# Two chained attentions and a gated MLP on one core: the first softmax's sums taken as a tiled product, its scale applied to the packed rows, and new instruction lists

## The chip, the cores and the metric

The kernel runs on one core of one Trainium2 chip. A core has five engines with a list of instructions each: TensorE (PE: matmuls, with its weight loads shown as PEld), VectorE (DVE), ScalarE (ACT), GpSimd (POOL) and SyncE (SP, which here issues nearly all DMAs). An engine works through its list strictly in order and waits at semaphores for what others produce. SBUF is the on-chip memory with 128 partitions; PSUM holds matmul results in banks of 512 float32 columns. The metric is the device time of one execution in microseconds (us), the median of several runs.

## The reference

Shapes: batch 8, heads 8, sequence 576, head size 64, 32 packed queries p per head; MLP 512 to 2048 to 512.

```python
def sm_attn(qq, kk, vv):
    s = scale * np.matmul(qq, kk.transpose(0, 1, 3, 2))
    s = s - np.max(s, axis=-1, keepdims=True)
    a = np.exp(s)
    a = a / (np.sum(a, axis=-1, keepdims=True) + 1e-09)
    return np.matmul(a, vv)
p_packed = sm_attn(p, k, v)
out = sm_attn(q, p_packed, p_packed)

h = x @ w_in
g = h * (1.0 / (1.0 + np.exp(-beta * h)))
return (g @ w_out).astype(np.float32)
```

Here x is the attention's output with the heads of one token laid side by side. In the first attention 32 packed queries look at 576 keys; in the second, 576 queries look at the 32 packed rows, which serve as keys and as values.

## The kernel before

The work goes batch by batch, b from 0 to 7. In the lists below, each entry is a step: a name, the batch, and an index.

For each batch: `cast` turns k, v and q into bfloat16; `tr` and `trr` transpose k and q, on TensorE for batches 0 and 1 and by a DMA for the later ones; `s1` and `s1r` are the first scores, with the keys on the partitions; `e1` and `e1r` are their exponentials, kept in `E1T`. A tile of `E1T` has 256 columns: the 8 heads by 32 packed queries, in the order (r, c, j), where head = 2c + r and j is the query. `z1` adds the exponentials over the keys and `i1` inverts the sums. `pun` multiplies v by the exponentials (its result is `pp_ps`); `pp` brings that to SBUF as bfloat16, still without the division by the sums. `s2` (and `s2r` for the 64 remaining tokens) are the second scores from `pp` and q; `e2`, `e2r` their exponentials; `z2`, `l2`, `n2` and `A2` divide by the second sums, by a logarithm and an exponential on ScalarE and a product on VectorE.

The product of `pp` with w_in is taken before the second attention is applied: `w` (b, n), n from 0 to 3, multiplies a quarter of w_in by `pp`, and `W` (b, m) scales the result with beta into `W_bf`. Then `h` is one 128-row block of the hidden layer (two matmuls of 512 columns), `g` its SiLU, `hr` and `gr` the same for the remaining 64 tokens. `o` is the last product for batches 0 and 1 and for the remaining rows; for batches 2 to 7 the last product is done by seven block products instead of eight (`p` and `P` on TensorE, the sums `S` on VectorE, the reads `R..` on VectorE and ScalarE). `take` and `add` bring results to SBUF; `store` writes them out.

`z1` before takes the exponentials as the stationary operand, 128 of the 256 columns at a time, and one column of ones as the moving operand. Its result is a column for r = 0 and one for r = 1, with a sum on each partition (c, j). In that form the inverse of a sum is a value per partition for everything that has (c, j) on its partitions: the second scores and the product `w`. So `e2` and `e2r` take it (times 1/8) as ScalarE's scale operand, L695 and L700, and `W` takes it as the scalar of a three-operand instruction, L795.

The `s2`, `s2r` and `w` matmuls use the array as eight tiles of 64 rows by 32 columns (`pos=` gives the tile); everything else uses it whole. A run of neighbouring steps of the tiled kind is called a burst here.

What order the work has is written out by hand in `SEQUENCE`, one list of steps for each of the five engines. The `Planner` doesn't choose the order; it runs through the lists with assumed durations, and uses them for one thing alone: in the first 60 us, where it reckons that TensorE would stand still, it puts in "fill" matmuls, which multiply an identity by itself and whose result nobody reads (`keep_warm`, shown as o_ps<-identr). `TILED` names the steps that the planner takes for tiled.

PSUM banks are shared: `h` and `o` have two each, and all attention steps (s1, z1, pun, s2, z2, w) take turns in four. Weights w_in and w_out arrive in blocks of 1 MB through three staging slots: a block's load is issued when the casts of the third block before it are done. SP's list holds the loads, the DMA transposes and the stores in one order.

All matmuls are recorded at one line, that of the helper `mm` (L382), and PE transposes at L387, so the profile tells them apart by tile names: z_ps<-ones,E1T is z1, z_ps<-E2T,bones is z2, s_ps<-qT,pp is s2, s_ps<-pT,kT is s1, pp_ps is pun.

Of the kernel before, what the change touches and what calls it, by code (L numbers as in the profile page):

```python
# [21 lines left out]
NC = 4  # L22
# [22 lines left out]
TILED = {"w": 1, "s2": 1}  # L45
# [22 lines left out]
        ("o", 0, 3, 9), ("o", 0, 3, 11), ("s2", 1, 1), ("w", 1, 1), ("o", 0, 2, 9), ("o", 0, 3, 13), ("z2", 1, 2),
        ("o", 0, 2, 11), ("w", 1, 2), ("o", 0, 2, 13), ("h", 1, 2), ("o", 0, 2, 15), ("h", 1, 1), ("o", 0, 3, 15),
        ("h", 1, 0), ("w", 1, 3), ("h", 1, 5), ("h", 1, 3), ("p_tr", 1), ("h", 1, 4), ("o", 1, 0, 1), ("h", 1, 11),  # L70
        ("p_tr", 0), ("h", 1, 6), ("o", 1, 0, 3), ("h", 1, 8), ("o", 1, 1, 1), ("h", 1, 9), ("h", 1, 10),
        ("o", 1, 1, 3), ("hr", 0, 0), ("h", 1, 7), ("o", 1, 0, 5), ("o", 1, 1, 5), ("s1r", 2), ("hr", 0, 1),
        ("s1", 2, 1), ("o", 1, 0, 7), ("s1", 2, 0), ("h", 1, 15), ("o", 1, 0, 9), ("o", 1, 0, 11), ("o", 1, 1, 7),
        ("z1", 2), ("pun", 2, 0), ("o", 1, 1, 9), ("pun", 2), ("o", 1, 1, 11), ("h", 1, 13), ("h", 1, 12),
        ("w", 2, 0), ("w", 2, 1), ("h", 1, 14), ("o", 1, 1, 13), ("hr", 1, 0), ("o", 1, 0, 13), ("o", 1, 0, 15),
        ("hr", 1, 1), ("o", 1, 1, 15), ("s2", 2, 0), ("w", 2, 2), ("o", 1, 2, 1), ("o", 1, 2, 3), ("z2", 2, 0),
        ("o", 1, 2, 5), ("z2", 2, 1), ("o", 1, 3, 1), ("s2", 2, 1), ("o", 1, 2, 7), ("o", 1, 2, 9), ("o", 1, 3, 3),
        ("o", 1, 2, 11), ("o", 1, 2, 13), ("o", 1, 2, 15), ("o", 1, 3, 5), ("o", 1, 3, 7), ("z2", 2, 2), ("h", 2, 0),
        ("h", 2, 6), ("o", 1, 3, 9), ("s1r", 3), ("o", 1, 3, 11), ("h", 2, 1), ("s1", 3, 1), ("o", 1, 4, 1),
        ("o", 1, 3, 13), ("s1", 3, 0), ("o", 1, 4, 3), ("w", 2, 3), ("o", 1, 4, 5), ("o", 1, 4, 7), ("h", 2, 2),  # L80
        ("o", 1, 4, 9), ("o", 1, 3, 15), ("z1", 3), ("pun", 3, 0), ("h", 2, 7), ("h", 2, 3), ("pun", 3),
        ("o", 1, 4, 11), ("h", 2, 8), ("h", 2, 11), ("w", 3, 0), ("w", 3, 1), ("h", 2, 9), ("h", 2, 10),
        ("o", 1, 4, 13), ("o", 1, 4, 15), ("h", 2, 5), ("h", 2, 13), ("w", 3, 2), ("w", 3, 3), ("h", 2, 4),
        ("h", 2, 12), ("p", 2, 1, 0), ("p", 2, 1, 1), ("h", 2, 15), ("h", 2, 14), ("p", 2, 1, 2), ("P", 2, 1),
        ("hr", 2, 0), ("p", 2, 2, 0), ("hr", 2, 1), ("p", 2, 2, 1), ("p", 2, 2, 2), ("s2", 3, 0), ("s2", 3, 1),
        ("P", 2, 2), ("p", 2, 6, 0), ("p", 2, 6, 1), ("z2", 3, 0), ("p", 2, 6, 2), ("P", 2, 6), ("z2", 3, 1),
        ("z2", 3, 2), ("p", 2, 5, 0), ("p", 2, 5, 1), ("s1r", 4), ("s1", 4, 1), ("p", 2, 5, 2), ("s1", 4, 0),
        ("P", 2, 5), ("p", 2, 7, 0), ("p", 2, 7, 1), ("p", 2, 7, 2), ("P", 2, 7), ("p", 2, 3, 0), ("h", 3, 15),
        ("p", 2, 3, 1), ("z1", 4), ("h", 3, 14), ("p", 2, 3, 2), ("h", 3, 1), ("pun", 4, 0), ("h", 3, 0),
        ("p", 2, 4, 0), ("h", 3, 9), ("P", 2, 3), ("h", 3, 8), ("pun", 4), ("p", 2, 4, 1), ("h", 3, 5), ("h", 3, 2),  # L90
        ("w", 4, 0), ("w", 4, 1), ("h", 3, 3), ("h", 3, 7), ("p", 2, 4, 2), ("P", 2, 4), ("h", 3, 11), ("h", 3, 10),
        ("w", 4, 2), ("w", 4, 3), ("h", 3, 4), ("h", 3, 6), ("p", 3, 1, 0), ("p", 3, 1, 1), ("h", 3, 13),
        ("h", 3, 12), ("p", 3, 1, 2), ("P", 3, 1), ("p", 3, 2, 0), ("p", 3, 2, 1), ("hr", 3, 0), ("p", 3, 2, 2),
        ("hr", 3, 1), ("P", 3, 2), ("s2", 4, 0), ("s2", 4, 1), ("p", 3, 6, 0), ("p", 3, 6, 1), ("p", 3, 6, 2),
        ("z2", 4, 0), ("p", 3, 5, 0), ("P", 3, 6), ("z2", 4, 1), ("p", 3, 5, 1), ("p", 3, 5, 2), ("z2", 4, 2),
        ("P", 3, 5), ("s1r", 5), ("s1", 5, 0), ("s1", 5, 1), ("p", 3, 7, 0), ("p", 3, 7, 1), ("h", 4, 10),
        ("p", 3, 7, 2), ("P", 3, 7), ("z1", 5), ("pun", 5, 0), ("p", 3, 3, 0), ("p", 3, 4, 0), ("p", 3, 4, 1),
        ("h", 4, 7), ("h", 4, 2), ("p", 3, 3, 1), ("pun", 5), ("p", 3, 3, 2), ("h", 4, 14), ("h", 4, 15),
        ("p", 3, 4, 2), ("P", 3, 3), ("h", 4, 0), ("h", 4, 1), ("P", 3, 4), ("w", 5, 0), ("w", 5, 1), ("h", 4, 11),
        ("h", 4, 12), ("o", 3, 4, 1), ("o", 3, 4, 3), ("h", 4, 13), ("h", 4, 8), ("o", 3, 4, 5), ("o", 3, 4, 7),  # L100
        ("h", 4, 3), ("h", 4, 6), ("w", 5, 2), ("w", 5, 3), ("hr", 4, 0), ("h", 4, 4), ("o", 3, 4, 9),
        ("o", 3, 4, 11), ("h", 4, 9), ("h", 4, 5), ("o", 3, 4, 13), ("o", 3, 4, 15), ("s2", 5, 0), ("s2", 5, 1),
        ("p", 4, 1, 0), ("p", 4, 1, 1), ("p", 4, 1, 2), ("hr", 4, 1), ("z2", 5, 0), ("P", 4, 1), ("p", 4, 2, 0),
        ("z2", 5, 1), ("p", 4, 2, 1), ("p", 4, 2, 2), ("P", 4, 2), ("p", 4, 6, 0), ("p", 4, 6, 1), ("p", 4, 6, 2),
        ("P", 4, 6), ("p", 4, 5, 0), ("h", 5, 10), ("h", 5, 11), ("p", 4, 5, 1), ("p", 4, 5, 2), ("h", 5, 7),
        ("h", 5, 3), ("P", 4, 5), ("p", 4, 7, 0), ("p", 4, 7, 1), ("z2", 5, 2), ("s1r", 6), ("p", 4, 7, 2),
        ("s1", 6, 0), ("p", 4, 3, 0), ("s1", 6, 1), ("p", 4, 3, 1), ("P", 4, 7), ("p", 4, 3, 2), ("h", 5, 15),
        ("h", 5, 13), ("P", 4, 3), ("p", 4, 4, 0), ("p", 4, 4, 1), ("h", 5, 9), ("h", 5, 1), ("p", 4, 4, 2),
        ("z1", 6), ("h", 5, 8), ("h", 5, 0), ("pun", 6, 0), ("pun", 6), ("h", 5, 2), ("h", 5, 14), ("w", 6, 0),
        ("w", 6, 1), ("h", 5, 4), ("h", 5, 5), ("P", 4, 4), ("w", 6, 2), ("h", 5, 6), ("h", 5, 12), ("p", 5, 1, 0),  # L110
        ("p", 5, 1, 1), ("hr", 5, 0), ("hr", 5, 1), ("w", 6, 3), ("s2", 6, 0), ("p", 5, 1, 2), ("P", 5, 1),
        ("p", 5, 2, 0), ("p", 5, 2, 1), ("p", 5, 2, 2), ("P", 5, 2), ("z2", 6, 0), ("s2", 6, 1), ("p", 5, 6, 0),
        ("p", 5, 6, 1), ("p", 5, 6, 2), ("z2", 6, 1), ("P", 5, 6), ("z2", 6, 2), ("s1r", 7), ("s1", 7, 0),
        ("p", 5, 5, 0), ("p", 5, 5, 1), ("s1", 7, 1), ("p", 5, 5, 2), ("p", 5, 7, 0), ("p", 5, 7, 1), ("p", 5, 7, 2),
        ("P", 5, 5), ("h", 6, 2), ("h", 6, 12), ("P", 5, 7), ("p", 5, 3, 0), ("p", 5, 3, 1), ("h", 6, 4),
# [235 lines left out]
class Kernel:  # L351
# [153 lines left out]
    def plan_attention(self, b):  # L505
# [838 lines left out]
```

## Time and profile before

| what | value |
|---|---|
| median of 3 runs (lowest, highest) | 246.91 us (246.82, 247.11) |
| the profiled execution's time | 246.91 us |
| its span, first to last instruction | 245.1 us |
| granted TensorE clock, mean | 1.000 |
| busy: PE, ACT, DVE, POOL | 231.1, 178.8, 148.7, 58.8 us |
| bytes moved by DMA | 54.13 MB, mean 221 GB/s |
| fill matmuls (o_ps<-identr) | 132, 11.7 us busy |

The profile's page has first the busy time of each engine, then the span in 40 slices of some 6.1 us with a digit for the busy tenths of each; then the DMA queues, the chain of waits that ended last, and the costliest groups of instructions (line, engine, operation, output<-inputs, shape, count; then busy us, mean ns of one, and the idle time before them with what ended it). The timeline lists instructions in order of time, equal neighbours merged: start, length, engine, line, operation, count, and in brackets the idle time before and what released it. Lengths of matmuls overlap each other, since the array is a pipeline; what a matmul costs is the distance from its start to the start of the next.

### The profile page before, as it was taken

The page shows a single profiled execution, that of the slowest core. Times are in us where ns is not written, and L with a number is a line of the kernel's source. Part 1 is how long each engine was busy: PE and PEld are TensorE (multiplying, and loading weights), DVE is VectorE, ACT ScalarE, POOL GpSimd, SP SyncE. Part 2 cuts the span into 40 slices and gives each one's busy share as a digit, 9 for nine tenths or more (in the row PEclk, how much of TensorE's full clock was granted, in tenths as well). Part 3 has the DMA queues.
Part 4 walks back from the last instruction along what each step waited for, and adds up shares of the span by engine and source line. Part 5 has one row for each costly group of instructions (what it writes and reads, how often), then busy time and mean ns, then how long its engine had stood idle before and what let it go on. Part 6 is the DMA issues. An engine that isn't in the chain of part 4 may idle for free.

```text
span 245.1 us, 5810 instructions
## 1 busy us (share of the span) xinstructions
PE 231.1 (94%) x2429; PEld 151.0 (62%) x2429; DVE 148.7 (61%) x239; ACT 178.8 (73%) x317; POOL 58.8 (24%) x75
## 2 busy tenths in 40 slices
PE   3997779989999999999999999999999999999992
PEld 3985434633464444787578744886587557667870
DVE  6455566676907937872788376843993368813521
ACT  2486959887797897797779767988798769766210
POOL 4002313206443034207430541061305000000000
PEclk9999999999999999999999999999999999999999
DMA  6999999999989999999999999995993141004024
GB/s 195 298 332 376 305 356 312 366 256 292 199 270 143 277 301 344 183 292 285 280 176 304 325 276 187 337 228 133 195 289 75 36 171 45 1 0 174 0 77 140
DMA packets 74826, 54.13 MB, mean 221 GB/s; under 512 B 42688, under 2 KB 68304, under 8 KB 74800
## 3 DMA queue, kind: packets, MB, share of 16 engines
q1 hardware_dynamic: 74496, 53.68, 85.0%
q8 instruction: 19, 0.31, 0.5%
q10 hardware_dynamic: 304, 0.07, 0.2%
q14 instruction: 7, 0.06, 0.1%
HBM read 37.23 MB, written 9.44 MB: 190 GB/s over the span
## 4 chain that ended last, share of the span: by engine, by line
PE 73%; DMA 16%; issue 5%; POOL 3%; SPq 1%; DVE 0%; POOLq 0%
PE o_ps L382 42%; PE h_ps L382 19%; DMA kr<-in_k_dram 6%; DMA k<-in_k_dram 5%; DMA v<-in_v_dram 5%; PE hr_ps L382 3%; PE w_ps L382 3%; PE s_ps L382 2%; PE z_ps L382 2%; PE pp_ps L382 1%; POOL k_bf L463 1%; POOL p_dup L1172 1%; POOL w_in_bf L1251 1%; SPq L434 0%; PE pT_ps L387 0%
## 5 line engine op out<-in xcount | busy, mean ns | idle before, releaser
L827 ACT ACTIVATE g_main<-h_ps 128x512 bf16<-128x512 f32 x128 | 71.6, 595 | 29.7 <-PE h_ps L382 29.5
L382 PEld LDWEIGHTS <-g_main 128*128 128x128 bf16 x608 | 57.0, 98 | 27.0 <-issue 4.0
L382 PE MATMUL o_ps<-w_out_bf,g_main 128*128 128x256 bf16 (+1 forms) x416 | 72.2, 306 | 0.9 <-ACT w_out_bf L1262 0.5
L382 PE MATMUL h_ps<-A2T,W_bf 128*128 128x512 bf16 x256 | 69.8, 380 | 0.9 <-DVE A2T L736 0.6
L795 DVE SCALAR_TENSOR_TENSOR W_bf<-w_ps,rz,beta_bc 128x512 bf16<-128x512 f32 x64 | 45.1, 745 | 14.5 <-PE w_ps L382 14.4
L382 PEld LDWEIGHTS <-W_bf 128*128 128x128 bf16 x512 | 32.2, 98 | 22.7 <-issue 5.5
L397 ACT ACT_TABLE_LOAD x24 | 30.8, 1283 | 1.1 <-PEq L1328 0.7
L1043 DVE TENSOR_TENSOR o_sb<-o_ps,o_sb 128x512 f32<-128x512 f32 x18 | 12.4, 690 | 24.2 <-PE o_ps L382 21.5
L382 PE MATMUL o_ps<-w_sum,g_main 128*128 128x256 bf16 x192 | 25.9, 273 | 0.0
L382 PE MATMUL o_ps<-w_sum,g_sum 128*128 128x256 bf16 x192 | 24.8, 273 | 0.0
L463 POOL CAST v_bf<-v 128x1024 bf16<-128x1024 f32 x14 | 15.0, 1082 | 37.9 <-DMA v<-in_v_dram 29.0
L382 PEld LDWEIGHTS <-g_sum 128*128 128x128 bf16 x192 | 18.1, 98 | 4.1 <-issue 0.5
L463 POOL CAST q_bf<-q 128x1024 bf16<-128x1024 f32 x12 | 13.2, 1116 | 28.2 <-DMA q<-in_q_dram 14.9
L463 POOL CAST k_bf<-k 128x1024 bf16<-128x1024 f32 x14 | 15.2, 1101 | 16.7 <-DMA k<-in_k_dram 9.7
L382 PE MATMUL o_ps<-w_out_bf,g_rem 128*128 128x512 bf16 x64 | 16.3, 380 | 0.0
L382 PE MATMUL o_ps<-identr 128*128 128x128 bf16 x132 | 11.7, 244 | 3.7 <-DVE bones L1108 3.7
L1045 ACT COPY o_sb<-o_ps 128x512 f32<-128x512 f32 x12 | 7.0, 587 | 10.0 <-PE o_ps L382 10.0
L382 PE MATMUL w_ps<-w_in_bf,pp 64*32 64x512 bf16 x256 | 11.9, 383 | 2.3 <-POOL w_in_bf L1251 1.3
L382 PEld LDWEIGHTS <-identr 128*128 128x128 bf16 x132 | 9.5, 111 | 5.7 <-DVE bones L1108 3.7
L382 PEld LDWEIGHTS <-pp 64*32 64x32 bf16 x384 | 4.3, 89 | 13.5 <-issue 9.3
L695 ACT ACTIVATE E2T<-s_ps,rz 128x512 bf16<-128x512 f32 x16 | 10.7, 688 | 1.8 <-PE s_ps L382 1.3
L736 DVE TENSOR_TENSOR A2T<-E2T,rz 128x512 bf16<-128x512 bf16 x16 | 11.1, 691 | 1.4 <-ACT rz L731 1.4
(99 smaller groups left out, 261.1 us busy)
## 6 DMA issues: line engine op xcount, KB each, us to landing
out_dram<-o_sb SPq DMA_DIRECT2D x14, 512.0 KB, 3.6
k<-in_k_dram SPq DMA_DIRECT2D x6, 1024.0 KB, 8.9
q<-in_q_dram SPq DMA_DIRECT2D x6, 1024.0 KB, 9.1
v<-in_v_dram SPq DMA_DIRECT2D x6, 1024.0 KB, 8.1
w_in<-in_moe_w_in_dram SPq DMA_DIRECT2D x4, 1024.0 KB, 10.3
w_out<-in_moe_w_out_dram SPq DMA_DIRECT2D x4, 1024.0 KB, 10.5
k<-in_k_dram SPq DMA_DIRECT2D x4, 512.0 KB, 9.8
q<-in_q_dram SPq DMA_DIRECT2D x4, 512.0 KB, 7.6
```

The source lines that it names most:

```text
L382: return self.nc.tensor.matmul(out, lhsT, rhs, start=start, stop=stop, tile_position=pos, skip_group_check=True)
L397: self.nc.scalar.preload_act_table_set(SETS[mode])
L463: self.copy[engine](o[:, 0:2048].rearrange("p (t h d) -> p h t d", t=4, h=8)[:, h], t[:, 0:2048].rearrange("p (h t d) -> p h t d", h=8, t= ...
L695: nc.scalar.activation(st[b, "E2"][:, i, 0:SM], st[b, "s2", i][:], AF.Exp, scale=st[b, "rz1"][:, 2 + i : 3 + i])
L736: nc.vector.tensor_tensor(part(st[b, "A2"], i), part(st[b, "E2"], i), st[b, "rz2"][:, i] if i < 2 else st[b, "rz2r"][:], ALU.mult)
L795: nc.vector.scalar_tensor_tensor(st[b, "W"][:, r, cols], st[b, "w", m][:], st[b, "rz1"][:, r : r + 1], self.beta_bc[:, cols], op0=ALU.mult ...
L827: nc.scalar.activation(st[b, "g"][:, ft, :], st[b, "h", ft][:], AF.Silu)
L1043: nc.vector.tensor_tensor(o, x, o, ALU.add)
L1045: self.copy[engine](o, x)
L1172: self.copy[engine](self.p_dup[0:LATER, :, e, :], self.p32[0:LATER])
L1251: self.copy[engine](self.w_in_bf[:, c, 512 * n : 512 * n + 512], self.t["w_in", n][:, c])
```

## The change

Four things change in what is computed where, and all five lists are new.

1. `z1` swaps its operands. The ones (128 x 64) are now the stationary operand and the exponentials the moving one, 128 columns at a time; r = 0 goes to the array's columns 0 to 63 and r = 1 to columns 64 to 127, as two tiles of 128 x 64. The result is a sum for each (c, j) along the columns, the same on all 64 partitions of a half. There are ten matmuls as before.
2. `i1` inverts 128 columns instead of 2, and its second instruction (times 1/8) goes.
3. `pp` multiplies by the inverse on its way to SBUF, in two VectorE instructions; before, it was two copies, on VectorE for six batches and on ScalarE for batches 1 and 7. `pp` now waits for `i1`, and `e2`, `e2r` and `W` no longer do. `e2` and `e2r` get the constant scale 1/8, and `W` becomes a two-operand product.
4. The columns of `E1T` are in the order (c, r, j): s1 writes its columns side by side, `e1r` and `pun` read them so, and `z1` picks the columns of one r.

```diff
-TILED = {"w": 1, "s2": 1}
+TILED = {"w": 1, "s2": 1, "z1": 2}
...
         def sums1():
             st[b, "z1"] = ps = self.att("z1_ps")
-            for r in range(2):
-                for t in range(5):
+            for t in range(5):
+                for r in range(2):
                     self.mm(
-                        ps[:, r : r + 1],
-                        E()[:, t, 128 * r : 128 * r + 128],
-                        self.ones64[:, 0:1],
+                        ps[64 * r : 64 * r + 64, 0:128].rearrange("p (c j) -> p c j", c=NC),
+                        self.ones64[:],
+                        E()[:, t, :].rearrange("p (c r j) -> p r c j", c=NC, r=2)[:, r],
                         start=(t == 0),
                         stop=(t == 4),
+                        pos=(0, 64 * r),
                     )
 
         def invert1():
-            st[b, "rz1"] = rz = self.sm.tile([128, 4], f32, tag="rz", name="rz1")
-            nc.vector.reciprocal(rz[:, 0:2], st[b, "z1"][:, 0:2])
-            nc.vector.tensor_scalar_mul(rz[:, 2:4], rz[:, 0:2], SCALE)
+            st[b, "rz1"] = rz = self.sm.tile([128, 128], f32, tag="rz1", name="rz1")
+            nc.vector.reciprocal(rz[:], st[b, "z1"][:, 0:128])
...
-        def pack(engine):
+        def normalize1():
             st[b, "pp"] = pp = self.sm.tile([128, NC, NP], bf16, tag="pp", name="pp")
             for r in range(2):
                 h = slice(64 * r, 64 * r + 64)
-                self.copy[engine](
-                    pp[h], st[b, "pun"][h, 0:256].rearrange("p (c r j) -> p r c j", c=NC, r=2)[:, r]
-                )
+                nc.vector.tensor_tensor(
+                    pp[h],
+                    st[b, "pun"][h, 0:256].rearrange("p (c r j) -> p r c j", c=NC, r=2)[:, r],
+                    st[b, "rz1"][h].rearrange("p (c j) -> p c j", c=NC),
+                    ALU.mult,
+                )
...
-        self.task(("pp", b), {"DVE": 0.45, "ACT": 0.5}, None, pack, [last], rank + 4, ends=[pun])
+        self.task(("pp", b), "DVE", 0.6, normalize1, [i1, last], rank + 4, ends=[pun])
...
-                st[b, "E2"][:, i, 0:SM], st[b, "s2", i][:], AF.Exp, scale=st[b, "rz1"][:, 2 + i : 3 + i]
+            nc.scalar.activation(st[b, "E2"][:, i, 0:SM], st[b, "s2", i][:], AF.Exp, scale=SCALE)
...
-            nc.vector.scalar_tensor_tensor(
-                st[b, "W"][:, r, cols], st[b, "w", m][:], st[b, "rz1"][:, r : r + 1], self.beta_bc[:, cols],
-                op0=ALU.mult, op1=ALU.mult,
+            nc.vector.tensor_tensor(
+                st[b, "W"][:, r, cols], st[b, "w", m][:], self.beta_bc[:, cols], ALU.mult
             )
```

The lists hold the same steps (but for which engine takes a cast or a copy) in another order. TensorE's list around `z1` of batch 2, and VectorE's around `i1` of batches 4 and 6:

```diff
-        ("z1", 2), ("pun", 2, 0), ("o", 1, 1, 9), ("pun", 2), ("o", 1, 1, 11), ("h", 1, 13), ("h", 1, 12),
+        ("z1", 2), ("pun", 2, 0), ("o", 1, 1, 9), ("pun", 2), ("h", 1, 13), ("o", 1, 1, 11), ("h", 1, 12),
         ("w", 2, 0), ("w", 2, 1),
...
-        ("R22+", 2), ("R12+", 2), ("i1", 4), ("pp", 4), ("W", 4, 0),
+        ("R22", 2), ("i1", 4), ("R22+", 2), ("pp", 4), ("A2", 3, 2),
...
-        ("R22+", 4), ("R12+", 4), ("i1", 6), ("pp", 6), ("A2", 5, 2),
+        ("R22+", 4), ("R12+", 4), ("i1", 6), ("A2", 5, 2), ("pp", 6),
```

SP's list up to the last block of w_in; `ld_out` is a block of w_out, (1, "k") the keys of batch 1, ("ld", 0, "q", 2) the last 64 tokens of q of batch 0:

```diff
-        ("ld", 0, "v", 0), ("ld", 0, "q", 1), ("ld", 0, "v", 1), ("ld", 0, "v", 2), ("ld_in", 0), ("ld_in", 1),
-        ("ld_out", 0), ("ld", 1, "k", 0), ("ld", 1, "k", 1), ("ld_in", 2), ("ld", 1, "k", 2), ("ld", 0, "q", 2),
-        ("ld_out", 1), ("ld_in", 3),
+        ("ld", 0, "q", 0), ("ld", 0, "q", 1), ("ld", 0, "v", 1), ("ld", 0, "v", 2), ("ld_in", 0), ("ld_in", 1),
+        ("ld", 0, "q", 2), ("ld", 1, "k", 0), ("ld", 1, "k", 1), ("ld_out", 0), ("ld_in", 2), ("ld", 1, "k", 2),
+        ("ld_out", 1), ("ld_in", 3),
```

In the built programs TensorE has 132 fill matmuls before and 119 after (119 and 115 of them ahead of `w` (0, 2)), and the array's tiling changes 64 times before and 84 times after (58 and 76 times from `w` (0, 2) on). The casts of the first block of w_in were one on GpSimd and one on VectorE and are now both on VectorE; those of the third were both on VectorE and are now one on ScalarE and one on VectorE.

## The prediction

> **What bounds the kernel now.** I read the page's shares first, then TensorE's work by stretches, then TensorE's instructions in order of time. Start with the shares and the stretches (columns: length, then busy us and count of PE, PEld, DVE, ACT, POOL, clock, DMA share, GB/s).
>
> ```profile
> PE 231.1 (94%) x2429; PEld 151.0 (62%) x2429; DVE 148.7 (61%) x239; ACT 178.8 (73%) x317; POOL 58.8 (24%) x75
> PE   3997779989999999999999999999999999999992
> 20.00:30.00 10.00, 6.95 (x90) 4.81 (x90) 6.17 (x11) 7.71 (x13) 3.45 (x3) 1.00 1.10 341
> 62.00:100.00 38.00, 37.88 (x394) 19.05 (x395) 24.22 (x42) 31.71 (x55) 14.27 (x19) 1.00 1.12 245
> 100.00:150.00 50.00, 50.00 (x576) 34.88 (x574) 34.38 (x51) 39.09 (x73) 17.09 (x20) 1.00 1.13 269
> ```
>
> From 62 us on TensorE is busy all the time (37.88 of 38.00, then 50.00 of 50.00) at full granted clock, while VectorE has a third and ScalarE a fifth of the same stretch free. Only the opening is loose (6.95 of 10.00 between 20 and 30 us). So what the late part costs is what TensorE has to issue; a busy share of 100% can still hold pauses of the array, because each matmul's end is modelled. I therefore read TensorE's timeline from start to start (columns: start, length, instruction):
>
> ```profile
> 127.25 0.60 PE L382 MATMUL o_ps<-w_out_bf,g_main 128*128 128x256 bf16 x4
> 127.69 0.63 PE L382 MATMUL hr_ps<-A2T,W_bf 128*128 128x64 bf16 x16
> 128.16 0.60 PE L382 MATMUL o_ps<-w_out_bf,g_main 128*128 128x256 bf16 x4
> 128.69 0.41 PE L382 MATMUL s_ps<-qT,pp 64*32 64x512 bf16 x8
> 128.91 0.21 PE L382 MATMUL s2r_ps<-qT,pp 64*32 64x64 bf16 x8
> 129.06 1.49 PE L382 MATMUL o_ps<-w_sum,g_sum 128*128 128x256 bf16 x12
> ...
> 133.05 0.27 PE L382 MATMUL s1r_ps<-pT,kT 128*128 128x128 bf16 x2
> 133.16 0.63 PE L382 MATMUL s_ps<-pT,kT 128*128 128x64 bf16 x16
> ...
> 135.81 0.39 PE L382 MATMUL z_ps<-ones,E1T 128*128 128x1 bf16 x10
> 136.06 0.63 PE L382 MATMUL pp_ps<-E1T,v_bf 128*128 128x64 bf16 x16
> ...
> 142.29 0.60 PE L382 MATMUL o_ps<-w_sum,g_main 128*128 128x256 bf16 x4
> 142.82 0.62 PE L382 MATMUL w_ps<-w_in_bf,pp 64*32 64x512 bf16 x16
> 143.37 1.04 PE L382 MATMUL h_ps<-A2T,W_bf 128*128 128x512 bf16 x4
> ```
>
> Four o matmuls take 0.44 when a full-array product follows (127.25 to 127.69) and 0.53 when a tiled one does (128.16 to 128.69, 142.29 to 142.82): entering the 64x32 tiling costs 0.09. Eight tiled s2 matmuls together take 0.22 (128.69 to 128.91), what one 512-column matmul takes alone, so tiles do run at once. Sixteen w matmuls should take 0.43 but the h product starts after 0.55: leaving costs 0.11. So each change of tiling costs about 0.10 on the engine that sets the end. The sums z1 cost 0.25 (135.81 to 136.06) for ten weight loads with ten one-column matmuls, and no change of tiling. One 128-column matmul costs 0.055 (s1r, two in 0.11).
>
> **The change, part by part.**
>
> *Changes of tiling.* z1 moves from the whole array to two 128x64 tiles, so each of the eight becomes a burst of its own: in no place of the new list does a z1 stand next to an s2 or w. Counting bursts in the two engine lists, with the fills that the build puts between, from w(0,2) on (the point where, below, the two kernels have done the same work): 29 bursts before, 38 after: seven z1 and two more of s2 and w. That is 18 more changes x 0.099 = **+1.8**, all on TensorE, which has no idle time to hide them in. The trace has no 128x64 tiling, so the price of the 14 z1 changes lies between 0 (column tiling alone needs no pause) and 0.11 each; I take the 64x32 price, the nearest row.
>
> *The z1 matmuls.* Ten of one column in 0.25 become ten of 128 columns, five pairs on two column tiles. If a pair overlaps as the eight tiles of s2 do: 5 x 0.055 = 0.28; if not at all: 0.55. I take 0.28, since every tiled burst of the trace overlaps fully: 7 x 0.03 = **+0.2** (bound +2.1). The Trainium skill, "TensorEngine Tiling (Array Packing)", section "Performance Considerations", recommends just this for a small moving side, swapping the operands and tiling the columns, for up to twice the speed; by it z1 would fall from 0.25 to 0.125 and the sum lose about 0.9 (an estimate). The rows don't support it: the old form already ran at 25 ns per matmul, the new one streams 128 columns.
>
> The same page, section "Restrictions and Gotchas", says that column tiling excludes the fast weight load, which speaks against the change: if ten slower loads of ones64 set the pace, the sum would go toward the unoverlapped end. The w bursts, with tiled loads too, show no such cost (8 load-and-matmul pairs in 0.22), but their loads have 32 columns, not 64.
>
> *VectorE and ScalarE.* Prices from these groups:
>
> ```profile
> L795 DVE SCALAR_TENSOR_TENSOR W_bf<-w_ps,rz,beta_bc 128x512 bf16<-128x512 f32 x64 | 45.1, 745 | 14.5 <-PE w_ps L382 14.4
> L1043 DVE TENSOR_TENSOR o_sb<-o_ps,o_sb 128x512 f32<-128x512 f32 x18 | 12.4, 690 | 24.2 <-PE o_ps L382 21.5
> L637 DVE RECIPROCAL rz<-z_ps 128x2 f32<-128x2 f32 x8 | 1.3, 167 | 8.8 <-PE z_ps L382 8.6
> L1229 DVE RECIPROCAL rbeta<-bcol_ps 128x16 f32<-128x16 f32 x1 | 0.2, 239 | 0.0
> ```
>
> W becomes a two-operand product: 64 x (745 - 690) = -3.5 on VectorE. The reciprocal grows from 2 to 128 columns: (239 - 167) / 14 = 5.1 ns a column, so 0.17 + 126 x 0.0051 = 0.81, in place of 0.17 and the 0.27 multiply behind it: 8 x 0.38 = +3.0. The pp products stay near the 0.29 of the pp casts (a product and a copy of 128x512 both take 690), but all 16 are now on VectorE, 4 having been ScalarE's: +1.2. VectorE +0.7 in sum; ScalarE loses these 4 casts (1.0) and gets a constant scale in 16 exps of 128x512 (688 to the 598 of the first softmax's exp, -1.4). Both lie beside TensorE's work and I count **0**. The cover is this: pp now waits for the reciprocal. From z1's end a pp needs 0.2 (hop) + 0.81 + 0.6 + 0.3 (hop) = 1.9 before w may start. The tightest dense place, batch 2, has pun 0.46, o 0.43, pun 0.12, h, o, h 1.30 between: 2.3. If the cover fails, w stands on TensorE, and everything behind it in that list.
>
> *Lists and loads.* All five lists are new. Up to w(0,2) both have 18 h and o matmuls done and all beta rows; w(0,2) waits for the third w_in block:
>
> ```profile
> 19.49 1.56 POOL L1251 CAST w_in_bf<-w_in 128x1024 bf16<-128x1024 f32 x1 [10.49 <-DMA w_in<-in_moe_w_in_dram]
> 21.08 0.37 SPq L1245 DMA_DIRECT2D w_in<-in_moe_w_in_dram  x1
> 32.96 0.41 PE L382 MATMUL w_ps<-w_in_bf,pp 64*32 64x512 bf16 x8 [0.89 <-DVE w_in_bf L1251]
> ```
>
> SP issues that load when the cast of the first block has ended (21.05) and frees its slot. In the new lists that cast is two on VectorE (0.70 each), so it frees about 0.2 sooner; the 0.13 MB of q's rest moved ahead in SP's list costs about 0.4 at 341 GB/s; its own casts go to two engines in place of one after the other (-0.3). Sum 0; the later z1 chain of batch 0 (+0.24) ends well before w_in arrives. w_out's first block goes behind k of batch 1 (1 MB, 3 us later), and the first o products stand one product later in the list. After w(0,2) the old kernel still stands 1.35 us (0.23, 0.17, 0.54, 0.41) and covers about 1.0 us with 13 fills near 48 us; the new build has 4 fills there. Those waits are set by casts and landings that I can't place to half a microsecond: between -2.4 (all gone) and +1.5 (as many again, less the fills); I take **0**. The end is the same: eight o(7,4) products, one take, one store.
>
> Sum: +1.8 + 0.2 = +2.0 on a span of 245.1. The profiled run is the median itself (246.91; 1.8 lies outside the span), so **248.9**.
>
> **Rivals.** (1) *z1's pairs do not overlap* (no overlap, or slow weight loads): 7 x 0.28 more: 250.9. For it: no 128x64 tiling in the trace. Against: full overlap of the eight tiles in s2 and w.
> (2) *The reciprocal becomes the wait.* VectorE's list is strict order; in batches 3, 4, 5 and 6 another operation (take, R22+, A2) stands between reciprocal and pp. If w or s2 stands for one such operation, about 0.7, in four of seven batches: +2.8: 251.7. Against: those batches have over 3 us of products between z1 and w.
> (3) *Column tiling needs no pause*: 14 x 0.1 less: 247.5. For it: only the columns are divided here, the contraction keeps its 128 rows. Against: nothing measured but that every 64x32 burst pays on both sides.
> (4) *Faster.* The new order leaves TensorE no stand between w(0,2) and 62 us: 1.35 + 1.0 + 0.6 (w_in's casts parallel and early) = 2.95 less: 246.0. It decides from 2.5 us saved. For it: fewer fills after w(0,2), 4 for 13. Against: DMA is full there (share 1.10), so landings do not move by reordering alone.
>
> **How the numbers follow.** Forecast (slower by about 2) 0.60; rival 1 0.12; rival 2 0.07; rival 3 0.10; rival 4 0.11. The forecast's own range, by its waits, is 247.9 to 249.9. Leaving out the ends of rivals 4 and 2, the range is 247.0 to 251.2. A measurement can tell 0.2% (0.5 us) from no change. Faster: rival 4, 0.11. Within 0.2%: the lower part of rival 3 and the forecast's own edge, 0.08. Slower: the rest, 0.81.
>
> **What would show it.** Each step in TensorE's timeline after: an o or h product ahead of z1 with 0.09 more than its own time, z1 itself 0.28 (or 0.55) long, 0.1 behind it; w(0,2) near 33 us; reciprocals near 0.8; TensorE still full from 62 us on; no w or s2 that waits for pp. I am wrong if z1's neighbours pay nothing, if w waits for pp, or if w(0,2) starts more than 1 us from 33.

## The result, and the profile after

| | kernel before | kernel after |
|---|---|---|
| median of 4 runs (lowest, highest) | 246.91 us (246.82, 247.11) | 250.36 us (250.11, 251.47) |
| profiled execution, its span | 246.91 us, 245.1 us | 250.11 us, 248.3 us |

The ratio is 1.0147, with an interval of 1.0116 to 1.0178: the change costs 2.9 to 4.4 us by this comparison. A second comparison on another chip session, 12 runs against 35, gave 250.54 to 249.0, a ratio of 1.0067 (1.004 to 1.0094). Both intervals lie above 1; they do not agree on how much slower it is, and the section on the prediction comes back to that. Where medians are compared below, they are from one session.

The page of the kernel after, its shares and its clock by slices:

```profile
PE 235.3 (95%) x2416; PEld 151.9 (61%) x2416; DVE 156.0 (63%) x235; ACT 175.5 (71%) x312; POOL 63.8 (26%) x76
PEclk9997979999999999999999999999999999999998
```

The same kernel by stretches (start and end, length; busy us and count of PE, PEld, DVE, ACT, POOL; clock, DMA share, GB/s):

```profile
20.00:30.00 10.00, 9.28 (x86) 6.63 (x87) 7.42 (x14) 7.30 (x12) 3.06 (x3) 0.83 1.08 341
62.00:100.00 38.00, 38.00 (x379) 18.48 (x378) 22.48 (x34) 31.59 (x55) 16.76 (x19) 1.00 1.14 256
100.00:150.00 50.00, 50.00 (x551) 34.43 (x550) 35.36 (x49) 38.54 (x72) 16.48 (x19) 1.00 1.05 267
```

TensorE is as full from 62 us on as before (38.00 of 38.00, 50.00 of 50.00), so the busy share can't show what the change costs; that takes distances from start to start. The clock of 0.83 from 20 to 30 us belongs to this one execution: the three others of the first session were granted 0.997 to 0.999 and took 250.30 to 251.47, no less than the 250.11 of the profiled one. It is not where the time went.

What a sum z1 costs now, TensorE in order of start (start, length, instruction; z1 is z_ps<-E1T,ones):

```profile
43.73 0.59 PE L383 MATMUL o_ps<-w_out_bf,g_main 128*128 128x512 bf16 x2
44.25 0.47 PE L383 MATMUL z_ps<-E1T,ones 128*64 128x128 bf16 x10
44.66 0.82 PE L383 MATMUL h_ps<-A2T,W_bf 128*128 128x512 bf16 x3
```

Two o products of 512 columns should take 0.43, and z1 starts after 0.52: entering costs 0.09. The h product starts 0.41 after z1's first matmul; with 0.10 for leaving, the ten matmuls have 0.31 of their own. From 0.25 before to 0.50 now, each z1 is 0.25 dearer.

The operations of VectorE that changed (instances, then busy us and mean ns of one, then idle time before them with its releaser):

```profile
L795 DVE TENSOR_TENSOR W_bf<-w_ps,beta_bc 128x512 bf16<-128x512 f32 x64 | 41.0, 684 | 11.6 <-PE w_ps L383 11.4
L736 DVE TENSOR_TENSOR A2T<-E2T,rz 128x512 bf16<-128x512 bf16 x16 | 13.2, 845 | 5.2 <-ACT rz L731 5.2
L638 DVE RECIPROCAL rz<-z_ps 128x128 f32<-128x128 f32 x8 | 7.6, 951 | 6.5 <-PE z_ps L383 6.5
L659 DVE TENSOR_TENSOR pp<-pp_ps,rz 64x128 bf16<-64x128 f32 x16 | 4.6, 288 | 10.7 <-PE pp_ps L383 10.4
```

The reciprocal takes 0.951, W 0.684, pp 0.288. A2, which the change does not touch, has a mean of 0.845. And these are TensorE's waits in the kernel after (what waited, for whom; us in total, times, longest):

```profile
PE o_ps L383 <- DVE bones L1107: 3.7, 1, 3.7
PE w_ps L383 <- DVE w_in_bf L1250: 2.0, 1, 2.0
PE krT_ps L388 <- DVE k_bf L474: 1.8, 1, 1.8
PE pp_ps L383 <- DVE v_bf L474: 0.3, 1, 0.3
PE h_ps L383 <- DVE A2T L736: 0.2, 1, 0.2
PE o_ps L383 <- DVE o_sb L1044: 0.2, 1, 0.2
```

No w or s2 waits for pp. But one h waits for an A2 and one o for a read of PSUM, both behind 185 us, where TensorE had not waited for VectorE in the kernel before. The timeline there, all engines:

```profile
185.40 1.94 POOL L464 CAST v_bf<-v 128x1024 bf16<-128x1024 f32 x1 [19.18 <-DMA v<-in_v_dram]
...
186.36 2.97 DVE L736 TENSOR_TENSOR A2T<-E2T,rz 128x512 bf16<-128x512 bf16 x2
...
187.29 1.49 POOL L464 CAST q_bf<-q 128x1024 bf16<-128x1024 f32 x1
...
188.74 1.49 POOL L464 CAST v_bf<-v 128x1024 bf16<-128x1024 f32 x1
188.77 0.38 PE L383 MATMUL h_ps<-A2T,W_bf 128*128 128x512 bf16 x1
...
189.38 0.38 PE L383 MATMUL h_ps<-A2T,W_bf 128*128 128x512 bf16 x1 [0.24 <-DVE A2T L736]
...
189.98 0.60 PE L383 MATMUL o_ps<-w_out_bf,g_main 128*128 128x256 bf16 x4 [0.23 <-DVE o_sb L1044]
```

Two A2 products take 2.97 together, while GpSimd casts batch 7's v and q at the same time, also slower than usual (1.94 and 1.49). The two matmuls of one h, 0.216 apart elsewhere, start 0.61 apart, and the o behind them stands again. I call this the clash. It goes back to an issue on SP: the new list has the load of batch 7's v behind a store (`("store", 9)`) and issues it at 178.65, so its landing, and with it GpSimd's casts, fall on the A2 products of batch 6. (In the kernel before it was issued at 158.45.)

### The profile page after: what moved, and what is told of

The parts are those of the page before. It is cut to its first block, busy times and chain, and to the rows that moved or that the text cites. A ratio compares the mean times of both kernels' runs of the same rounds, so it can differ in the third digit from the quotient of the medians.

```text
span 248.3 us, 5792 instructions
## 1 busy us (share of the span) xinstructions
PE 235.3 (95%) x2416; PEld 151.9 (61%) x2416; DVE 156.0 (63%) x235; ACT 175.5 (71%) x312; POOL 63.8 (26%) x76
## 4 chain that ended last, share of the span: by engine, by line
PE 71%; DMA 17%; SPq 5%; DVE 3%; ACT 2%; issue 1%; POOL 1%; POOLq 0%; ACTq 0%
PE o_ps L383 39%; PE h_ps L383 20%; DMA k<-in_k_dram 12%; DMA v<-in_v_dram 4%; PE hr_ps L383 3%; PE w_ps L383 3%; SPq L435 2%; PE z_ps L383 2%; PE s_ps L383 2%; SPq L443 2%; PE pp_ps L383 1%; DVE A2T L736 1%; DMA out_dram<-o_sb 1%; ACT g_main L826 1%; SPq L1244 1%
## 5 line engine op out<-in xcount | busy, mean ns | idle before, releaser
L826 ACT ACTIVATE g_main<-h_ps 128x512 bf16<-128x512 f32 x128 | 72.7, 596 | 34.0 <-PE h_ps L383 33.7
L383 PE MATMUL o_ps<-w_out_bf,g_main 128*128 128x256 bf16 (+1 forms) x416 | 74.3, 309 | 0.2 <-DVE o_sb L1044 0.2
L383 PE MATMUL h_ps<-A2T,W_bf 128*128 128x512 bf16 x256 | 71.3, 380 | 0.4 <-DVE A2T L736 0.2
L795 DVE TENSOR_TENSOR W_bf<-w_ps,beta_bc 128x512 bf16<-128x512 f32 x64 | 41.0, 684 | 11.6 <-PE w_ps L383 11.4
L464 POOL CAST q_bf<-q 128x1024 bf16<-128x1024 f32 x14 | 17.3, 1241 | 33.9 <-DMA q<-in_q_dram 29.1
L383 PE MATMUL o_ps<-w_out_bf,g_rem 128*128 128x512 bf16 x64 | 16.9, 379 | 0.0
L464 POOL CAST k_bf<-k 128x1024 bf16<-128x1024 f32 x13 | 14.4, 1120 | 9.6 <-DMA k<-in_k_dram 8.1
L736 DVE TENSOR_TENSOR A2T<-E2T,rz 128x512 bf16<-128x512 bf16 x16 | 13.2, 845 | 5.2 <-ACT rz L731 5.2
L383 PE MATMUL o_ps<-identr 128*128 128x128 bf16 x119 | 10.6, 252 | 3.7 <-DVE bones L1107 3.7
L719 ACT ACTIVATE rz<-z_ps 128x512 f32<-128x512 f32 x16 | 9.3, 594 | 4.2 <-PE z_ps L383 4.0
```

What stands on the lines that cost most here:

```text
L383: return self.nc.tensor.matmul(out, lhsT, rhs, start=start, stop=stop, tile_position=pos, skip_group_check=True)
L464: self.copy[engine](o[:, 0:2048].rearrange("p (t h d) -> p h t d", t=4, h=8)[:, h], t[:, 0:2048].rearrange("p (h t d) -> p h t d", h=8, t= ...
L719: nc.scalar.activation(st[b, "rz2"][:, i], ps[:], AF.Ln)
L736: nc.vector.tensor_tensor(part(st[b, "A2"], i), part(st[b, "E2"], i), st[b, "rz2"][:, i] if i < 2 else st[b, "rz2r"][:], ALU.mult)
L795: nc.vector.tensor_tensor(st[b, "W"][:, r, cols], st[b, "w", m][:], self.beta_bc[:, cols], ALU.mult)
L826: nc.scalar.activation(st[b, "g"][:, ft, :], st[b, "h", ft][:], AF.Silu)
```

## The experiments

All runs are read with the same landmarks on TensorE: the start of w(0,2), the first z1 matmul of batch 2, and the start of the last matmul. The last distance, from z1 of batch 2 to the last matmul, is called the late stretch; TensorE is full in it, so it shows what the list costs, with such short stands as a clash brings. Where a difference lies is read from the distance between the first z1 matmuls of two batches.

| kernel | w(0,2) | z1 of batch 2 | last matmul | late stretch |
|---|---|---|---|---|
| before | 32.96 | 72.10 | 240.30 | 168.20 |
| before_again | 33.27 | 72.85 | 241.04 | 168.19 |
| after | 33.59 | 72.95 | 243.47 | 170.52 |
| after_again | 33.54 | 72.94 | 243.93 | 170.99 |
| new_sums_old_lists | 34.10 | 74.67 | 244.70 | 170.03 |
| old_sums_new_lists | 33.84 | 72.78 | 243.85 | 171.07 |
| earlier_v7_load | 32.79 | 71.32 | 241.05 | 169.73 |
| old_sums_new_lists_earlier_v7 | 33.77 | 72.96 | 241.72 | 168.76 |
| extra_full | 33.37 | 73.94 | 242.93 | 168.99 |
| extra_64x32 | 33.75 | 74.13 | 247.71 | 173.58 |
| extra_128x64 | 32.35 | 71.41 | 245.53 | 174.12 |
| extra_both | 32.47 | 71.72 | 249.68 | 177.96 |
| fewer_bursts | 34.71 | 73.95 | 243.55 | 169.60 |

### The kernel after once more

No edit; it serves as the partner of the next three kernels, which ran in the same session.

> The changed kernel once more. Its first profile showed the granted clock at 0.83 between 20 and 40 us, while three unprofiled executions took about the same time (250.3 to 251.5). If the throttled stretch matters to the end, a profile without it has its w(0,2) earlier and its time below 250.1; if that stretch only takes the place of a wait for the third w_in block, the time stays at 250.1 to 250.7 with a granted clock of 1.00.

Measured: 250.54 (249.37 to 251.39) against 249.0 (247.22 to 251.61), ratio 1.0067 (1.004 to 1.0094), clock 0.993. What follows: with the clock at 0.993 the kernel is no quicker than with 0.982, so the throttled stretch of the first profile is not the cause; and the difference to the kernel before is about half of the first session's.

### The new sums with the old lists

The code of the kernel after with the `SEQUENCE` of the kernel before; only what the new code demands is moved:

```diff
-ACT:  ("pp", 1) ... ("pp", 7)
+DVE:  ("pp", 1) ahead of ("T", 1, "q", 1);  ("pp", 7) behind ("i1", 7);  ("i1", 3) ahead of ("pp", 3)
```

> The new arithmetic in the old lists: z1 as a tiled product, the reciprocal of 128 columns, pp scaled; the lists are those of before, but that pp is on VectorE for all batches and stands behind the reciprocal. The tiling changes 80 times instead of 64. Theory (tiling changes on a full TensorE): 16 x 0.1 + 7 x 0.06 = +2.0, so about 248.9. Rival (the reciprocal as a wait): w or s2 waits for pp in several batches, over 250. Rival (it is the lists alone): no slower than 247.4.

Measured: 249.72, ratio 1.004 (1.001 to 1.0069); late stretch +1.83 over before. One w waits for pp, once (TensorE's waits in this kernel: us in total, times, longest):

```profile
PE w_ps L383 <- DVE pp L659: 0.2, 1, 0.2
```

This w is that of batch 4, and the place lost 0.6 of the 1.83 in all. Ahead of it an A2 was lengthened beside GpSimd's casts; the same kind of clash, at another place (the timeline of this kernel, GpSimd and VectorE):

```profile
111.14 3.34 POOL L464 CAST v_bf<-v 128x1024 bf16<-128x1024 f32 x2 [10.71 <-DMA v<-in_v_dram]
...
112.06 1.52 DVE L736 TENSOR_TENSOR A2T<-E2T,rz 128x512 bf16<-128x512 bf16 x1
...
114.11 0.92 DVE L736 TENSOR_TENSOR A2T<-E2T,rz 128x512 bf16<-128x512 bf16 x1
```

The new sums are not what made this w wait: in the run fewer_bursts below, whose code and lists are those of before up to batch 6, the same A2 took 1.52 too and the same w waited 0.28 for pp. So even in lists that were not made for it, the longer way over reciprocal and pp shows no wait of its own. That leaves 1.2 for the sums. Compared step by step with before, TensorE falls behind by 0.15 after the start of each of the six z1 and by 0.09 ahead of the five that lie inside the stretch, 1.35 in all.

### The old sums with the new lists

```diff
 # the code of the kernel before
-SEQUENCE = (the lists of the kernel before)
+SEQUENCE = (the lists of the kernel after)
```

> The old arithmetic in the new lists: z1 as one-column products on the whole array, no scale at pp, three-operand W. The tiling changes 68 times instead of 84. Theory: 16 x 0.1 + 7 x 0.06 = 2.0 less than the changed kernel, so about 248.4; what is left over 246.9, some 1.5, then belongs to the lists (four more changes, 0.4, and their waits, 1.1). Rival (all of it is the sums): 246.9 to 247.3. Rival (all of it is the lists): 250 or more.

Measured: 249.14, ratio 1.0018 (0.9991 to 1.0044), which is not to be told from no change; its profiled execution took 250.55, with a late stretch of +2.87. The lists alone thus have the clash, without any of the new arithmetic (its timeline; first VectorE's and TensorE's rows near 138 us, then all engines near 188):

```profile
135.32 2.05 DVE L1014 TENSOR_TENSOR g_main<-g_main,g_sum 128x2048 bf16<-128x2048 bf16 x1
...
138.03 0.60 PE L383 MATMUL o_ps<-w_out_bf,g_main 128*128 128x256 bf16 x4 [0.56 <-DVE o_sb L1046]
...
185.95 2.03 POOL L464 CAST q_bf<-q 128x1024 bf16<-128x1024 f32 x1
...
187.00 2.96 DVE L737 TENSOR_TENSOR A2T<-E2T,rz 128x512 bf16<-128x512 bf16 x2
...
188.95 0.38 PE L383 MATMUL h_ps<-A2T,W_bf 128*128 128x512 bf16 x1
...
190.01 0.38 PE L383 MATMUL h_ps<-A2T,W_bf 128*128 128x512 bf16 x1 [0.68 <-DVE A2T L737]
```

Here the two matmuls of h start 1.06 apart. A second clash stands in front: near 138 us a product S takes 2.05 in place of 1.22 beside GpSimd's casts, and an o stands 0.56 for the read of its PSUM bank that VectorE has behind it. The median lies 1.4 below the profiled execution, which is one of the longest of its twelve; how often the others had these stands can't be read.

### Batch 7's v loaded earlier

The kernel after; SP's list alone is changed, by one entry:

```diff
-("tr", 6, "q", 0), ("store", 8), ("store", 3, 4), ("tr", 7, "k", 0), ("store", 9), ("ld", 7, "q", 2), ("ld", 7, "v", 0),
+("tr", 6, "q", 0), ("ld", 7, "v", 0), ("store", 8), ("store", 3, 4), ("tr", 7, "k", 0), ("store", 9), ("ld", 7, "q", 2),
```

> The changed kernel with one step moved: SP issues the load of batch 7's v right behind the DMA transpose of batch 6's q, instead of behind store 9, so that GpSimd casts it some 13 us sooner. In the changed kernel's trace these casts run at 185.4 to 190.2, and two A2 products of VectorE at the same time take 1.53 and 1.52 in place of 0.69; h(6) then waits, TensorE loses 0.8. Theory (GpSimd and VectorE hinder each other): A2 of batch 6 takes 0.7 again, that stand goes, and the time falls by about 0.8, to 249.6. Rival (A2 is slow for another reason): A2 stays at 1.5 and the time at 250.4.

Measured: 248.87, ratio 0.9991 (0.9961 to 1.002), against 1.0067 (1.004 to 1.0094) for the kernel after in the same session: the intervals are apart. The load is issued at 164.74, the casts run when no A2 does, the two A2 take 1.29, and the two matmuls of h stand side by side (its timeline, all engines):

```profile
164.74 0.53 SPq L435 DMA_DIRECT2D v<-in_v_dram  x1
...
171.62 1.04 POOL L464 CAST v_bf<-v 128x1024 bf16<-128x1024 f32 x1 [6.75 <-PE pp_ps L383]
...
184.72 1.29 DVE L736 TENSOR_TENSOR A2T<-E2T,rz 128x512 bf16<-128x512 bf16 x2
...
187.13 0.59 PE L383 MATMUL h_ps<-A2T,W_bf 128*128 128x512 bf16 x2
```

The late stretch is 0.79 shorter than that of after and 1.26 shorter than that of after_again. Only 0.79 of either is the edit's: from z1 of batch 6 to z1 of batch 7 both have 24.61, and this kernel 23.82. The other 0.47 of after_again was lost near 138 us, before the moved load is issued, where an o stood for VectorE (TensorE's timeline of after_again):

```profile
138.88 0.60 PE L383 MATMUL o_ps<-w_sum,g_main 128*128 128x256 bf16 x4 [0.20 <-DVE o_sb L1042]
```

So one load's place in SP's list was worth 0.8 us of the late stretch. This is shown by the edit, not only argued from the overlap.

### The same load in the kernel with the old sums

The edit above, made in old_sums_new_lists; what it leaves over before is the lists' own price without the clash.

> The old arithmetic in the new lists, with batch 7's v loaded earlier as well. In the trace of the old arithmetic in the new lists two A2 products took 1.52 in place of 0.69 at 187 to 190, and TensorE stood 1.2 there; from the first z1 matmul of batch 2 to the last matmul it took 171.07. Theory (the casts of GpSimd are the cause): that stretch falls by about 1.2, to 169.8, and the time to 248 to 249 beside a kernel before of 247 to 249. Rival: the stretch stays at 171.

Measured: late stretch 168.76, which is 2.31 less than with the clash and 0.57 above before; 248.08 against 247.59, ratio 1.004 (1.0 to 1.0079), in a session other than that of old_sums_new_lists. Of the 2.31, 1.23 fell between z1 of batches 6 and 7 (24.84, now 23.61), which is the edit's; the other 1.08 fell near 138 us, well ahead of the moved load's issue at 168.37: this execution had no stand there. Of the four changes of tiling that the new lists have more than the old ones, two lie in the late stretch; they make 0.2 of the 0.57. Another 0.3 are two stands of TensorE that the kernel with the new sums doesn't have, 0.21 ahead of an h behind pun of batch 2 (the pun of four matmuls takes 0.33 up to it, with the new sums 0.12) and 0.11 ahead of a z2 at 131.6.

### What a change of tiling costs

The kernel before, with 24 small matmuls between the two products of an h (every fourth h of batches 2 to 7); they write into PSUM that the h then overwrites. One kernel for each tiling, and the same matmul on the whole array as the control:

```diff
 def main(ft):
...
+            if b >= 2 and ft % 4 == 1:
+                self.mm(ps[:, 0:64], self.identr[:], self.identr[:, 0:64])                        # extra_full
+                self.mm(ps[0:32, 0:64], self.identr[0:64, 0:32], self.identr[0:64, 0:64], pos=(0, 0))  # extra_64x32
+                self.mm(ps[0:64, 0:64], self.identr[:, 0:64], self.identr[:, 0:64], pos=(0, 0))   # extra_128x64
+                # extra_both: the 128x64 one, then the 64x32 one
```

> The kernel before with 24 extra matmuls of 64 columns on the whole array, one ahead of every fourth h product of batches 2 to 7 (the result is overwritten by the h product behind it). No tiling changes are added. Every theory expects 24 x 0.029 = +0.7: 247.6. It is the control for the next three.

> The same 24 places, each with one matmul of 64 columns on a 64x32 tile: 46 tiling changes more than before. Theory (a change costs 0.10 wherever TensorE is full): +0.7 + 4.6, about 252.2. Rival (changes hide in the pipeline, their seeming cost is a matter of modelled ends): as the control, 247.6.

> The same with a 128x64 tile, as the new z1 has: 47 changes more. Theory (each change costs the same, whatever the tile): +0.7 + 4.7, about 252.3. Rival (dividing the columns alone needs no pause): 247.6.

> The same places with a 128x64 matmul and a 64x32 matmul side by side: 71 changes if going from one tiling to the other counts as one. Theory (every change of tiling costs 0.10): +0.7 + 0.7 + 7.1, about 255.4. Rival (only leaving and entering the whole array costs): about 253. This tells whether a z1 placed next to an s2 or w would have saved one change or two.

| kernel | time (before: 247.41) | ratio | late stretch over before | changes added | per change |
|---|---|---|---|---|---|
| extra_full | 248.28 | 1.0033 (0.9994 to 1.0073) | 0.79 | 0 | |
| extra_64x32 | 253.26 | 1.0246 (1.0184 to 1.0308) | 5.38 | 46 | (5.38 - 0.79) / 46 = 0.100 |
| extra_128x64 | 253.73 | 1.0272 (1.0209 to 1.0335) | 5.92 | 47 | (5.92 - 0.79) / 47 = 0.109 |
| extra_both | 256.2 | 1.0364 (1.0311 to 1.0418) | 9.76, 0.8 of it a clash | 71 | (9.76 - 0.8 - 2 x 0.79) / 71 = 0.104 |

In extra_both one h stood for an A2 that a cast had lengthened, which no change of tiling explains (its timeline, VectorE and TensorE):

```profile
112.53 1.46 DVE L736 TENSOR_TENSOR A2T<-E2T,rz 128x512 bf16<-128x512 bf16 x1
...
114.04 0.38 PE L382 MATMUL h_ps<-A2T,W_bf 128*128 128x512 bf16 x1 [0.79 <-DVE A2T L736]
```

The control has a stand of 0.12 of this kind at w of batch 4; without it the three prices are 0.102, 0.112 and 0.107. The medians say much the same: (253.26 - 248.28) / 46 = 0.108 and (253.73 - 248.28) / 47 = 0.116. TensorE's timeline in extra_128x64 (start, length, instruction):

```profile
142.65 0.59 PE L382 MATMUL h_ps<-A2T,W_bf 128*128 128x512 bf16 x2
143.17 0.22 PE L382 MATMUL h_ps<-identr 128*64 128x64 bf16 x1
143.32 0.60 PE L382 MATMUL h_ps<-A2T,W_bf 128*128 128x512 bf16 x2
```

And in extra_both:

```profile
144.73 0.59 PE L382 MATMUL h_ps<-A2T,W_bf 128*128 128x512 bf16 x2
145.26 0.35 PE L382 MATMUL h_ps<-identr 128*64 128x64 bf16 x2
145.54 0.60 PE L382 MATMUL h_ps<-A2T,W_bf 128*128 128x512 bf16 x2
```

The two h matmuls take 0.52 up to the small one in place of 0.43, and the small one 0.15 up to the next h, where on the whole array it took 0.79 / 24 = 0.033: 0.09 in, 0.12 out. With both tilings in a row (merged into one line here) the pair takes 0.28, that is 0.066 for the matmuls and 0.21 for two changes, from tile to tile and out. What follows: each change of tiling tried here costs 0.10 to 0.12, also the one that divides the columns alone, also from one tiling to the other.

### The kernel before once more

No edit; it shows how far the landmarks of one and the same code repeat.

> The kernel before once more, for its trace. Theory: from the first z1 matmul of batch 2 to the last matmul TensorE runs a fixed list without stands, so this stretch is 168.2 again (240.30 - 72.10 in the first trace), while the time until then differs from execution to execution with the landing of loads, by a microsecond or two. Rival: the late stretch differs as much as the time does.

Measured: 247.78 against 247.59, ratio 0.9983 (0.9928 to 1.0039) over its runs. The late stretch repeats to 0.01 us (168.20 and 168.19), as long as TensorE stands for no clash: the profile of fewer_bursts, next, loses 0.67 behind z1 of batch 4 with the same code and lists. The opening doesn't repeat: z1 of batch 2 starts 0.75 later than in the first profile (TensorE's timeline in this run):

```profile
72.85 0.39 PE L382 MATMUL z_ps<-ones,E1T 128*128 128x1 bf16 x10
```

### Fewer bursts

The kernel before with three tiled steps moved next to others, 4 changes of tiling less, and VectorE's W behind them:

```diff
-PE: ("w", 6, 2), ("h", 5, 6) ... ("w", 6, 3), ("s2", 6, 0) ... ("s2", 6, 1) ... ("w", 7, 2), ("o", 5, 4, 1) ... ("w", 7, 3)
+PE: ("w", 6, 2), ("w", 6, 3), ("h", 5, 6) ... ("s2", 6, 0), ("s2", 6, 1) ... ("w", 7, 2), ("w", 7, 3), ("o", 5, 4, 1)
-DVE: ("W", 6, 5), ("S", 5, 1), ("W", 6, 6), ("S", 5, 2), ("W", 6, 7) ... ("W", 7, 5), ("S", 6, 1) ... ("W", 7, 6), ("S", 6, 4), ("W", 7, 7)
+DVE: ("W", 6, 5), ("W", 6, 6), ("W", 6, 7), ("S", 5, 1), ("S", 5, 2) ... ("W", 7, 5), ("W", 7, 6), ("W", 7, 7), ("S", 6, 1) ... ("S", 6, 4)
```

> The kernel before with its bursts of batches 6 and 7 put together as in batches 3 to 5: w(6,3) next to w(6,2), s2(6,1) next to s2(6,0), w(7,3) next to w(7,2), and on VectorE W(6,6), W(6,7), W(7,6), W(7,7) ahead of the S sums. The tiling changes 60 times instead of 64. Theory: 4 x 0.1 less in the late stretch, 167.8 in place of 168.2, and the time lower by 0.4 (ratio 0.998). Rival: W is late or a PSUM bank is awaited, and the stretch is as long as before or longer.

Measured: 248.44 against 247.59, ratio 1.004 (1.0001 to 1.0079), late stretch 169.60: not shorter by 0.4 but longer by 1.4. A miss, and the timeline says why (VectorE and TensorE, from the profiled execution, at 250.17 one of its longest):

```profile
111.05 1.52 DVE L736 TENSOR_TENSOR A2T<-E2T,rz 128x512 bf16<-128x512 bf16 x1
...
120.81 0.95 PE L382 MATMUL w_ps<-w_in_bf,pp 64*32 64x512 bf16 x16 [0.28 <-DVE pp L659]
...
174.82 5.36 DVE L795 SCALAR_TENSOR_TENSOR W_bf<-w_ps,rz,beta_bc 128x512 bf16<-128x512 f32 x8
...
176.24 0.45 PE L382 MATMUL w_ps<-w_in_bf,pp 64*32 64x512 bf16 x8
176.94 0.37 PE L382 MATMUL w_ps<-w_in_bf,pp 64*32 64x512 bf16 x1 [0.25 <-DVE W_bf L795]
177.60 0.41 PE L382 MATMUL w_ps<-w_in_bf,pp 64*32 64x512 bf16 x7 [0.29 <-DVE W_bf L795]
```

The eight W of a batch now come in one row of 5.36 us on VectorE, and w(6,3) stands for the bank of PSUM that each of them frees: TensorE stands 0.25 and 0.29 for it. From z1 of batch 6 to z1 of batch 7 the kernel takes 0.94 more than before; behind that z1, where two of the four changes are saved and nothing stands, 0.20 less. So the saved changes pay, and the wait took more. The other 0.67 of the 1.4 was lost near 120 us, where a w of batch 4 waited for pp, a place that the edit does not touch: it is the clash of new_sums_old_lists in the code and lists of before.

No version beat the kernel before. The best of the new form is earlier_v7_load, which can't be told from it.

## Why the prediction was right and where it was not

The sign and the range held: 250.36 lies in 247.0 to 251.2. The forecast's own range, 247.9 to 249.9, did not hold the first session's median; 248.9 forecast +2.0, and that session measured +3.45, the second +1.54. That 250.36 lies inside at all is in part luck: the upper end was left for rivals 1 and 2, neither of which came true, and a cost that no rival named took its place. On the spans of the two profiled executions the difference is 248.3 - 245.1 = 3.2, which the landmarks divide into 0.85 up to z1 of batch 2, 2.32 in the late stretch, and 0.03 behind the last matmul.

*Changes of tiling, +1.8: right.* The price of 0.099 was read from the 64x32 bursts; for the 128x64 tiling the runs show 0.109, and 0.09 in and 0.10 out in the z1 of the kernel after. Rival 3, column tiling without a pause, is refuted.

*The z1 matmuls, +0.2: right.* Their own time is 0.31 by the trace, where 0.28 was expected for overlapping pairs and 0.55 for none; rival 1 is refuted. That column tiling excludes the fast weight load, as "TensorEngine Tiling (Array Packing)" of the Trainium skill has it in "Restrictions and Gotchas", does not show as a cost at this size. Nor does the gain of "Performance Considerations": ten matmuls that took 0.25 take 0.31 in the swapped and tiled form, and with its two changes 0.50.

*VectorE and ScalarE, 0: right in its effect, off in one size.* The reciprocal takes 0.951, not 0.81: its price by columns had been drawn out from 2 and 16 columns to 128. W (0.684) and pp (0.288) came as priced. The cover held all the same: TensorE waits for no pp, so rival 2 is refuted. VectorE's busy time rose by 7.3, not 0.7; reciprocals without the old multiply (+4.1), W (-3.9), pp (+1.2) and the lengthened A2 (+2.2, by 13.2 against 16 x 0.69) make 3.6 of that, and the rest was not followed up.

*Lists and loads, 0: this is the step that failed.* The prediction weighed the opening, up to 62 us, entry by entry, and took the late part of the lists for the same work in another order, but for the bursts. It did not follow SP's and GpSimd's lists past 62 us. There the issue of one load behind a store put casts beside two products, and TensorE stood 0.79. The late stretch adds up from one run to the next:

| step | from, to | us |
|---|---|---|
| new lists without the clash | before_again 168.19, old_sums_new_lists_earlier_v7 168.76 | +0.57 |
| new sums in them | 168.76, earlier_v7_load 169.73 | +0.97 |
| the clash | 169.73, after 170.52 | +0.79 |

The sum, 2.33, is the 2.32 of the two profiles. Of the prediction's 18 changes 13 lie in this stretch (two by s2 and w, eleven by z1; the other five lie between w(0,2) and z1 of batch 2), which is 1.29, and its six z1 matmul groups are 0.18: 1.47. The first two lines, 1.54 in all, came 0.1 over that, and the clash, which it had at nothing, stands wholly on top. That the new sums show 0.97 here and not the 1.35 that stands at the z1 themselves is mostly the two stands of 0.21 and 0.11 in the kernel with the old sums: where TensorE stood anyway, part of the price of z1 was hidden.

*The opening, 0.5 for five changes and one z1: not settled, and too fine to be.* w(0,2) started at 33.59, 0.59 from the 33 of the prediction. From there to z1 of batch 2 it was 39.36 in place of 39.14: +0.22 where the terms say 0.5. But the openings of the old code and lists in seven runs (before, before_again, fewer_bursts and the four extra kernels, whose edits lie behind this point) reach z1 of batch 2 between 71.41 and 74.13, at 72.87 in the mean, and the five with the new lists between 71.32 and 72.96, at 72.59. A difference of half a microsecond drowns in that. Rival 4, a faster opening, has nothing that speaks for it; the first pair of profiles happened to differ by 0.85 against the new kernel.

*What stays open.* The late stretch has +2.3 in the first profile of the kernel after and +2.8 in the second, which had the stand near 138 us as well. What decides whether a cast meets a product there, in one execution and not in another of the same kernel, was not followed up. The first session's medians say +3.45, the second's +1.54, and the difference of these is as large as the scatter of single openings. Which openings the unprofiled runs had can't be read, so the last microsecond is not assigned to anything.

## What to carry to other kernels

On an engine that is full, a small product in a tiling of its own costs its two changes, 0.2 us here, whatever it gains inside; count them in the list ahead of anything else, and the estimate holds to a few tenths. Then follow the queues that don't bound the kernel through the whole list and not only where there is slack: one load moved behind a store cost 0.8 us with the new sums and 1.2 with the old, as much as three to five z1. And before a difference in a stretch is explained, look at how far that stretch repeats with the same code: here to 0.01 us where TensorE is full and stands for no clash, with 0.5 to 1.1 us more where it did, and to 2.7 us where loads set the pace.

## What the runs showed that I had not expected

GpSimd's casts from float32 to bfloat16 and VectorE's products of two bfloat16 operands in SBUF slow each other: 0.69 became 1.52 for A2, and 1.04 became 1.94 and 2.03 for casts, where the two ran at once in the rows shown. It is no property of the new lists: two A2 near 187 us took 1.52 in fewer_bursts as well. It costs only where TensorE comes to wait for them. The Trainium skill, "SBUF — State Buffer", section "SBUF: two separate sides", has the rule behind these rows: a VectorE instruction with two inputs in SBUF and a GpSimd instruction that reads SBUF share a port pair that one of them holds for the whole instruction. The rows agree in kind: A2 with one cast ahead of it is 0.69 + 1.04 = 1.73 at most, and 1.52 was the longest in all thirteen traces. The operations that read PSUM on one side, such as W, kept their 0.684 in the mean.

From one tiling straight to the other costs as much as through the whole array: 0.104 per change with both in a row. So a z1 put next to a w has three changes in place of four, not two.

The same code on the same kind of chip had medians of 246.91, 249.0, 247.41 and 247.59 in four sessions, 0.8% apart. Only ratios within a session, or the late stretch of a trace, tell effects of the size of this one.
